# Attention followed by two gated MLPs on one core: key chunks in another order, weights-times-values products in three groups per head pair instead of five

## The chip, the cores and the metric

One core of a Trainium2 chip. The metric is the device time of one launch in microseconds. Engines are called as in the profile: PE (matmul) and PEld (its weight load), DVE, ACT, POOL, SP (the queue that issues the DMAs).

## What is computed

Attention over 4 batches of 8 heads with 576 positions and 64 channels, all in float32, then two MLPs on the 2304 x 512 result:

```python
scores = scale * np.matmul(q, k.transpose(0, 1, 3, 2))
thresh = np.max(scores, axis=-1, keepdims=True) - tau
scores = np.where(scores >= thresh, scores, -1000000000.0)
attn = softmax(scores)
x = np.matmul(attn, v)                  # heads side by side: 2304 x 512
x = (s * relu(x @ w_in) ** 2 + b) @ w_out
h = x @ w2_in;  out = (h * tanh(softplus(h))) @ w2_out
```

## The kernel before

The 32 heads are worked on as 16 **pairs** `pr` of two heads, four pairs to a batch. The 2 x 576 query rows of a pair make nine tiles `ti` of 128 rows (tile 4 holds the last 64 rows of both heads). `scores` (L238) computes one tile: four matmuls into `S` (eight for tile 4), a pass of DVE that gives the negated scores `ns` and their extremum, the exponential on ACT into `e`, and a `finish` on DVE one tile later that applies the threshold and sums. After tiles 1, 4 and 8 POOL divides the finished tiles by their sums (L279).

The weights must then be turned so that keys lie on the partitions. The 2 x 576 key columns of a pair are nine **chunks** of 128 (0 to 3 head 0, 5 to 8 head 1, chunk 4 the last 64 keys of head 0 beside the first 64 of head 1). `weights_t` (L285) transposes one chunk on PE: five transposes into the one PSUM buffer `T`, which ACT copies to an SBUF tile `te` (L302; six buffers). Chunk 4 needs all nine tiles of the pair. `product` (L305) multiplies with the values: `product(c)` takes chunk c for head 0 and chunk c + 5 for head 1 (chunk 4 for both), in four matmuls named A to D here: half 0 head 0, half 0 head 1, half 1 head 0, half 1 head 1. Each writes 64 of the 128 output columns of the array, head 0 the lower and head 1 the upper half. Every float32 matmul of this line leaves two rows in the trace, so a product leaves eight. The five products of a pair add up in one PSUM tile `pv`, which `split_x` (L316) takes out as `x[pr]`.

`attention` (L326) is a generator over tiles k. At tile k it emits the scores of tile k, the transposes of chunk number k - LAG, with LAG 7, and then the product that the chunk of the tile before made possible: after chunk 4 product 4, after chunks 5 to 8 products 0 to 3. At tiles 2 and 4 the next pair's keys and queries are prepared, at tile 8 the next pair's values are loaded.

The first MLP, `moe1` (L386), runs in blocks of one batch (four pairs): groups of 12 matmuls of 288 columns (L405). Its first block starts when `x[0]` to `x[3]` exist and splits its weights on the way (`wp`); later blocks load them (`w`). `run` (L584) interleaves the two generators by the estimated cost that each has emitted, attention inside `tc.high_priority(offset=200)` (L643). The fourth block of the first MLP and then the second MLP (`moe2`, L471) follow when attention is over.

What stands on each engine in which order is not the order of emission. The kernel is built with `schedule_with_timeline_sim=True` (L713): a scheduler gives each engine a fixed order of instructions, by readiness and priority.

Of the kernel before, what the change touches and what calls it, by code (L numbers as in the profile page):

```python
# [19 lines left out]
class Fused:  # L20
# [305 lines left out]
    def attention(self):  # L326

        nc = self.nc  # L330
        N = 9 * self.B * self.NP
        LAG = 7
        for n in "kq":
            self.load_raw(0, n)
        nc.sync.dma_start(self.tau_c, self.tau.partition_broadcast(P))
        nc.sync.dma_start(self.s_c, self.s.partition_broadcast(P))
        nc.sync.dma_start(self.b_c, self.b.partition_broadcast(P))
        self.load_raw(0, "v")
        for n in "kq":
            self.prep_qk(0, n)  # L340
        fin = todo = None
        tes = {}
        for k in range(N + LAG + 2):
            pr, ti = divmod(k, 9)
            if k < N:
                nxt = self.scores(pr, ti)
                if fin:
                    fin()
                fin = nxt
                yield 550  # L350
                if pr + 1 < self.B * self.NP and ti in (2, 4, 8):
                    if ti == 8:
                        self.load_raw(pr + 1, "v")
                    else:
                        self.prep_qk(pr + 1, "kq"[ti // 2 - 1])
                        yield 500
            elif fin:
                fin()
                fin = None
            j = k - LAG  # L360
            if 0 <= j < N:
                prj, ci = divmod(j, 9)
                tnew = self.weights_t(prj, ci)
                yield 550
            if todo:
                tp, tc, te = todo
                tes[tc] = te
                if tc == 4:
                    self.product(tp, 4, (te, te), True, False)
                    yield 490  # L370
                elif tc > 4:
                    self.product(tp, tc - 5, (tes[tc - 5], te), False, tc == 8)
                    yield 970
                if tc == 8:
                    self.split_x(tp)
            todo = (prj, ci, tnew) if 0 <= j < N else None


# [7 lines left out]
    def moe1(self, b):  # L386
# [79 lines left out]

        for layer, qf, part in ORDER:
            yield from (layer1, layer2)[layer](qf, part)


    def moe2(self, rest):  # L471
# [5 lines left out]
        def load(bi):  # L477
            n = 512 if bi < 4 else 256
            ys[bi] = [], [], n
            for e in range(4):  # L480
                for i, tag in enumerate(("xh", "xl")):
                    t = self.xp.tile([P, n], F32R, tag=tag, name=f"y2{bi}_{e}_{i}")
                    nc.sync.dma_start(t.bitcast(F32), self.yT[bi, e, i] if bi < 4 else self.yrem[e, i])
                    ys[bi][i].append(t)
# [42 lines left out]
        def output(bi, fc):  # L527
            gh, gl = gs.pop((bi, fc))
            n = ys[bi][2]
            w = self.w2["o", fc // 4]  # L530
            terms = [(gh, 0), (gh, 1), (gl, 0)]
            todo = [(i, t) for i in range(3) for t in range(n // 128)]
            if fc == 15:
                todo.sort(key=lambda it: it[1])
            for i, t in todo:
                if fc == 0 and i == 0:
                    outs[t] = self.op.tile([P, 512], F32, tag=f"o{t}", name=f"o{bi}_{t}")
                g, wl = terms[i]
                nc.tensor.matmul(outs[t], g[:, t * 128:t * 128 + 128], w[:, wl, fc % 4, :],  # L539
                                 start=(fc == 0 and i == 0), stop=(fc == 15 and i == 2))  # L540
            if fc < 15:
                return
            for t in range(n // 128):
                o = self.yp.tile([P, 512], F32, tag=f"y{t}", name=f"os{bi}_{t}")
                if t % 2:
                    nc.vector.tensor_copy(o, outs[t])
                else:
                    nc.scalar.copy(o, outs[t])
                if bi < 4:

                    dst = self.out[bi * 576:bi * 576 + 512, :].rearrange("(j c) e -> c j e", c=4)[t]
                    nc.sync.dma_start(dst, o)
                else:
                    for i in range(2):
                        r0 = (2 * t + i) * 576 + 512
                        nc.sync.dma_start(self.out[r0:r0 + 64, :], o[64 * i:64 * i + 64, :])

        LAG = 3
        load(0)
        prev = None  # L560
        n = len(work)
        for i in range(n + LAG):
            if i < n:
# [12 lines left out]
            prev = cur  # L576
            if i >= LAG:
                output(*work[i - LAG])
            for _ in range(2):
# [4 lines left out]
    def run(self, ctx):  # L584
# [5 lines left out]
        def pool(stack, name, bufs, **kw):  # L590
# [16 lines left out]
        att = self.attention()  # L607
        w1 = self.split_all([f for u in ORDER for i in range(2) for f in self.w1_pieces(u[0], u[1], 2 * u[2] + i)],
                            self.pre, ("raw", "ra"), bufs=3)
# [61 lines left out]

HALVES = [slice(0, 64), slice(64, 128)]

ORDER = [(0, 0, 0)]
for _q in range(4):
    ORDER += [(0, _q, 1)] + ([(0, _q + 1, 0)] if _q < 3 else []) + [(1, _q, 0), (1, _q, 1)]

# [40 lines left out]
```

## Time and profile before

| | |
|---|---|
| median of 3 runs | 1219.41 us (1215.17 to 1219.55) |
| the profiled execution | 1216.89 us |
| its span, first to last instruction | 1215.1 us |
| PE busy / PEld busy | 1153.1 us (95%) / 983.9 us (81%) |
| DVE / ACT / POOL busy | 868.4 / 592.5 / 657.9 us |
| mean granted clock of PE | 0.984 |
| first and last row of the products (L313) | 45.6 us and 656.7 us |
| first matmul of the first MLP | 131.5 us |

The profile is one execution. A row of the timeline merges neighbours of one kind on an engine; its first number is the start of the first, and the difference between two such starts is what the first kind took of PE. A matmul's own duration is longer than that, since matmuls overlap.

### The profile page before, as it was taken

What the parts mean: (1) busy time and instruction counts of PE and PEld (TensorE: products, weight loads), DVE (VectorE), ACT (ScalarE), POOL (GpSimd) and SP (SyncE); (2) the same over time, 40 slices, a digit from 0 to 9 for tenths busy, and PEclk for the clock granted to TensorE, in tenths of its full rate; (3) what the DMA queues carried; (4) which work ended last, traced back from release to release, by engine and by line L of the source; (5) the groups of instructions that cost most, each with busy time, mean ns of one, the idle gap of its engine ahead of it and who ended that gap; (6) DMA issues with size and microseconds to landing.
All of it is one profiled execution on the core that took longest, in us unless ns stands there. A gap on an engine that the chain in (4) does not pass through costs nothing.

```text
span 1215.1 us, 20290 instructions
## 1 busy us (share of the span) xinstructions
PE 1153.1 (95%) x7104; PEld 983.9 (81%) x7104; DVE 868.4 (71%) x1585; ACT 592.5 (49%) x1153; POOL 657.9 (54%) x841
## 2 busy tenths in 40 slices
PE   5888999999899999999999999988999999999998
PEld 4666878877788998988998999966888888888886
DVE  5888777878885465664652799799977676767865
ACT  4666666575555544455532575453433333344332
POOL 5566777786644343335431354346755655555654
PEclk8989999999999999999999999989999999999999
DMA  5556466576585445474433898842130020020000
GB/s 129 157 142 180 111 210 183 168 208 175 175 288 165 144 144 165 127 227 132 131 99 111 288 323 267 293 148 70 36 104 1 1 70 1 8 97 1 18 1 35
DMA packets 123671, 161.88 MB, mean 133 GB/s; under 512 B 57392, under 2 KB 78896, under 8 KB 123568
## 3 DMA queue, kind: packets, MB, share of 16 engines
q1 hardware_dynamic: 123568, 160.58, 43.2%
q8 instruction: 56, 0.92, 0.3%
q14 instruction: 47, 0.39, 0.1%
HBM read 107.48 MB, written 30.93 MB: 114 GB/s over the span
## 4 chain that ended last, share of the span: by engine, by line
PE 59%; DVE 13%; DMA 10%; POOL 6%; issue 5%; ACT 4%; SPq 2%; DVEq 0%; ACTq 0%; POOLq 0%
PE o L539 12%; PE h L405 11%; PE y L405 9%; PE pv L313 6%; PE hp L495 6%; PE hm L495 6%; PE S L254 5%; DMA wraw<-in_moe_w_in_dram 5%; PE T L291 4%; DMA wraw<-in_moe_w_out_dram 3%; DVE d L512 3%; POOL e L279 2%; DVE wa L67 2%; DVE wa L68 2%; DVE wa L66 2%
## 5 line engine op out<-in xcount | busy, mean ns | idle before, releaser
L512 DVE RECIPROCAL d<-d 128x512 f32<-128x512 f32 (+1 forms) x80 | 242.0, 3025 | 0.0
L405 PE MATMUL y<-gh,w 128*128 128x288 f32 x768 | 164.0, 299 | 2.7 <-DVE y L452 2.7
L405 PE MATMUL h<-xh,w 128*128 128x288 f32 x768 | 164.8, 300 | 1.3 <-DMA w<-w 1.0
L269 DVE SCALAR_TENSOR_TENSOR e<-ns,st,e 128x576 f32<-128x576 f32 x128 | 120.9, 948 | 45.5 <-ACT e L265 30.1
L260 POOL TENSOR_SCALAR st<-st,tau_c 128x1 f32<-128x1 f32 x144 | 60.9, 424 | 165.9 <-DVE ns L258 151.0
L539 PE MATMUL o<-w2o,g2h 128*128 128x512 f32 x576 | 149.7, 395 | 0.1
L258 DVE TENSOR_SCALAR_CACHE_REDUCE ns<-S 128x576 f32<-128x576 f32 x144 | 107.8, 752 | 55.6 <-PE S L254 54.9
L279 POOL TENSOR_SCALAR e<-e,st 128x576 f32<-128x576 f32 x128 | 126.4, 997 | 31.3 <-DVE st L274 28.9
L405 PEld LDWEIGHTS y<-gh,w 128*128 128x128 f32 x768 | 125.7, 188 | 10.2 <-issue 4.4
L265 ACT ACTIVATE e<-ns,st 128x576 f32<-128x576 f32 x128 | 98.9, 776 | 70.6 <-DVE ns L258 59.5
L405 PEld LDWEIGHTS h<-xh,w 128*128 128x128 f32 x768 | 125.7, 188 | 8.5 <-issue 5.7
L539 PEld LDWEIGHTS o<-w2o,g2h 128*128 128x128 f32 x576 | 107.1, 188 | 24.8 <-ACT g2h L519 0.6
L302 ACT COPY te<-T 128x576 f32<-128x576 f32 x144 | 91.3, 634 | 72.1 <-PE T L296 64.9
L429 POOL TENSOR_TENSOR gl<-rr,gh 128x288 fp32r<-128x288 f32 x96 | 81.0, 850 | 73.8 <-DVE rr L428 63.2
L495 PE MATMUL hp<-y,w2i 128*128 128x512 f32 (+1 forms) x480 | 113.6, 380 | 6.1 <-DVE t L511 6.0
L516 POOL TENSOR_TENSOR t<-t,d 128x512 f32<-128x512 f32 (+1 forms) x80 | 94.9, 1186 | 40.5 <-DVE d L512 40.3
L523 POOL TENSOR_TENSOR g2l<-t,g2h 128x512 fp32r<-128x512 f32 (+1 forms) x80 | 95.5, 1193 | 38.4 <-ACT g2h L519 36.1
L405 PE MATMUL y<-gl,w 128*128 128x288 f32 x384 | 113.7, 296 | 1.5 <-DVE gl L429 1.5
L405 PE MATMUL h<-xl,w 128*128 128x288 f32 x384 | 113.8, 296 | 0.0
L495 PE MATMUL hm<-y,w2i 128*128 128x512 f32 (+1 forms) x480 | 110.1, 373 | 3.1 <-DVE t L511 3.0
L254 PE MATMUL S<-KH,Q 128*128 128x288 f32 x320 | 101.6, 333 | 11.8 <-DVE ns L258 4.0
L291 PE MATMUL T<-ident,e 128*128 128x128 f32 x576 | 99.1, 281 | 13.6 <-ACT te L302 9.3
(100 smaller groups left out, 2481.8 us busy)
## 6 DMA issues: line engine op xcount, KB each, us to landing
w<-w SPq DMA_DIRECT2D x96, 512.0 KB, 4.2
wraw<-in_moe_w_in_dram SPq DMA_DIRECT2D x64, 256.0 KB, 3.9
w<-wp SPq DMA_DIRECT2D x32, 512.0 KB, 4.0
wraw<-in_moe_w_out_dram SPq DMA_DIRECT2D x64, 256.0 KB, 4.3
KH<-hik SPq DMA_DIRECT2D x60, 144.0 KB, 2.5
y<-yT SPq DMA_DIRECT2D x32, 256.0 KB, 4.1
KL<-lok SPq DMA_DIRECT2D x30, 144.0 KB, 2.7
rawq<-in_q_dram SPq DMA_DIRECT2D x32, 128.0 KB, 3.1
```

The costliest lines, as they stand in the source:

```text
L254: nc.tensor.matmul(so, Q[:, c0:c0 + 128], kt[:, ks], start=(i == 0), stop=(i == len(terms) - 1))
L258: nc.vector.tensor_scalar(ns.rearrange("p (h n) -> p h n", h=2), sv, -0.125, 3.0e38, op0=ALU.mult, op1=ALU.min, accum_out=nm[:, c1])
L265: nc.scalar.activation(e, ns, AF.Exp, bias=nm[:, c1], scale=-1.0)
L269: nc.vector.scalar_tensor_tensor(e, ns, nthr[:, c1], e, op0=ALU.is_le, op1=ALU.mult, accum_out=sm[:, c1])
L279: nc.gpsimd.tensor_scalar(t, t, rinv[:, j:j + 1], u[:, j:j + 1], op0=ALU.mult, op1=ALU.add)
L291: nc.tensor.transpose(T[:, i * 128:i * 128 + 128], self.es[pr, i, "pair"][:, o:o + 128], self.ident)
L405: nc.tensor.matmul(acc[:, :n], w[:, wl, c], rhs[c][xl][:, ts], start=(i == 0), stop=(i == 11))
L495: nc.tensor.matmul(hp[:, :n], w[:, wl, kc, fs], yy[kc], start=(i == 0), stop=(i == 11))
L512: nc.vector.reciprocal(d, d)
L516: nc.gpsimd.tensor_tensor(t, t, d, op=ALU.mult)
L523: nc.gpsimd.tensor_tensor(gl, t, gh.bitcast(F32), op=ALU.subtract)
L539: nc.tensor.matmul(outs[t], g[:, t * 128:t * 128 + 128], w[:, wl, fc % 4, :], start=(fc == 0 and i == 0), stop=(fc == 15 and i == 2))
```

## The change

The chunks of a pair are transposed in the order 0, 1, 4, 5, 6, 2, 7, 3, 8 instead of 0 to 8, nine tiles behind the scores instead of seven. The products are emitted in three groups: 4 and 0 after chunk 5, 1 and 2 after chunk 7, 3 after chunk 8. Values are loaded for the first two pairs at the start, and then for pair tp + 2 as soon as pair tp has been taken out of `pv`. `yield` costs of a product are 970 throughout (490 for product 4 before).

```diff
-        LAG = 7
+        LAG = 9
...
-        self.load_raw(0, "v")
+        for pr in range(2):
+            self.load_raw(pr, "v")
...
-                if pr + 1 < self.B * self.NP and ti in (2, 4, 8):
-                    if ti == 8:
-                        self.load_raw(pr + 1, "v")
-                    else:
-                        self.prep_qk(pr + 1, "kq"[ti // 2 - 1])
-                        yield 500
+                if pr + 1 < self.B * self.NP and ti in (2, 4):
+                    self.prep_qk(pr + 1, "kq"[ti // 2 - 1])
+                    yield 500
...
-                prj, ci = divmod(j, 9)
+                prj, cj = divmod(j, 9)
+                ci = CHUNKS[cj]
...
-                if tc == 4:
-                    self.product(tp, 4, (te, te), True, False)
-                    yield 490
-                elif tc > 4:
-                    self.product(tp, tc - 5, (tes[tc - 5], te), False, tc == 8)
+                for c in PRODUCTS.get(tc, ()):
+                    self.product(tp, c, (tes[c], tes[c + 5 if c < 4 else 4]), c == 4, c == 3)
                     yield 970
                 if tc == 8:
                     self.split_x(tp)
+                    self.load_raw(tp + 2, "v")
...
+CHUNKS = (0, 1, 4, 5, 6, 2, 7, 3, 8)
+PRODUCTS = {5: (4, 0), 7: (1, 2), 8: (3,)}
```

## Rows read from the trace of the kernel before

**Rows 1.** The page: busy time, share of the span and instructions of each engine.

```profile
PE 1153.1 (95%) x7104; PEld 983.9 (81%) x7104; DVE 868.4 (71%) x1585; ACT 592.5 (49%) x1153; POOL 657.9 (54%) x841
```

**Rows 2.** Windows: stretch, its us, busy us per engine (instructions), PE clock, DMA.

```profile
0.00:131.00 131.00, 103.69 (x620) 76.74 (x621) 100.27 (x278) 76.31 (x129) 76.56 (x134) 0.91 0.58 150
131.00:350.00 219.00, 205.06 (x1442) 175.57 (x1440) 171.70 (x430) 133.99 (x283) 160.34 (x226) 0.98 0.62 184
350.00:657.00 307.00, 306.15 (x2257) 272.86 (x2255) 165.51 (x404) 149.00 (x275) 122.94 (x174) 1.00 0.50 153
```

**Rows 3.** Waits of PE, 350 to 657 us: total us, times, longest us.

```profile
PE h L405 <- DMA w<-w: 0.4, 1, 0.4
PE T L291 <- ACT te L302: 0.4, 2, 0.2
```

**Rows 4.** The products: all by line L313; groups by line, 131 to 350 and 350 to 657 us.

```profile
L313 PE MATMUL pv<-te,rawv x640: 406/406/742, 45.6 to 656.7; 128*64 128x288 f32 x160
...
L313 PE MATMUL pv<-te,rawv 128*64 128x288 f32 x204 | 33.5, 419 | 0.0
...
L313 PE MATMUL pv<-te,rawv 128*64 128x288 f32 x280 | 47.3, 420 | 0.0
```

**Rows 5.** Timeline of PE, products of one pair: start us, us, what, number.

```profile
368.62 0.27 PE L296 MATMUL T<-ident,E 128*128 128x128 f32 x1
368.82 1.67 PE L313 MATMUL pv<-te,rawv 128*64 128x288 f32 x10
370.42 0.40 PE L405 MATMUL h<-xh,w 128*128 128x288 f32 x1
...
373.35 0.27 PE L296 MATMUL T<-ident,E 128*128 128x128 f32 x1
373.55 1.19 PE L313 MATMUL pv<-te,rawv 128*64 128x288 f32 x8
374.67 0.53 PE L405 MATMUL h<-xh,w 128*128 128x288 f32 x2
...
386.63 0.70 PE L313 MATMUL pv<-te,rawv 128*64 128x288 f32 x2
387.25 0.40 PE L254 MATMUL S<-KH,Q 128*128 128x288 f32 x1
```

**Rows 6.** Timeline of PE, a chunk's last transpose with no product behind it.

```profile
401.21 0.27 PE L296 MATMUL T<-ident,E 128*128 128x128 f32 x1
401.24 0.38 PE L405 MATMUL y<-gh,w 128*128 128x288 f32 x1
```

**Rows 7.** Timeline of PE, last products ahead of the first MLP.

```profile
127.97 1.19 PE L313 MATMUL pv<-te,rawv 128*64 128x288 f32 x8
...
130.36 1.18 PE L313 MATMUL pv<-te,rawv 128*64 128x288 f32 x6
131.47 0.41 PE L405 MATMUL h<-xh,wp 128*128 128x288 f32 x1
```

**Rows 8.** Timeline of ACT, the copy of chunk 5 of the pair of rows 5.

```profile
368.93 0.64 ACT L302 COPY te<-T 128x576 f32<-128x576 f32 x1
```

**Rows 9.** Timeline of SP, the load of the second pair's values.

```profile
15.79 0.95 SPq L173 DMA_DIRECT2D rawv<-in_v_dram  x2
```

**Rows 10.** Timeline of PE, transposes of a chunk 4.

```profile
405.44 0.27 PE L291 MATMUL T<-ident,e 128*128 128x128 f32 x1
...
406.07 0.27 PE L291 MATMUL T<-ident,e 128*128 128x128 f32 x1
```

**Rows 11.** Waits of PE, 130 to 350 us and 0 to 130 us.

```profile
PE S L254 <- DVE ns L258: 2.5, 5, 0.9
...
PE T L291 <- ACT te L302: 7.8, 9, 2.1
```

**Rows 12.** Waits of the SP queue, whole span.

```profile
SPq L173 <- PE pv L313: 9.7, 6, 4.2
```

## The prediction

> **What bounds the kernel now.** I began with busy time on the page: PE 95%, DVE 71% [rows 1]. A mean over stages decides nothing, so the windows came next. From 350 to 657 us PE is busy 306 of 307 us [rows 2], and the waits view finds 0.8 us there that PE spent on others [rows 3]: attention and the first MLP share an engine that never stops, and a microsecond added to it is a microsecond of the launch. From 131 to 350 us PE is idle 14 of 219 us, before that 27 of 131 [rows 2]; added work can hide there in part. The last product row starts at 656.7 [rows 4], so what follows is only shifted. The products lie 280 rows in the full stretch, 204 in the middle one, the rest of 640 before [rows 4]: at 40 rows per pair 7 pairs, 5 and 4.
>
> **What a run of products costs.** The timeline around one pair gives it, by starts. Without a product the next matmul starts 0.03 us after a chunk's last transpose [rows 6]. With one, the product starts 0.20 us after it, and the next matmul comes 1.60 us later behind ten rows, 1.12 behind eight, 0.62 behind two [rows 5], 1.11 behind six [rows 7]. Set against the 0.03, a run costs 1.77, 1.29, 0.79 and 1.28 us for ten, eight, two and six. Two full steps of PE more are 0.48 us (ten against eight), so a step is 0.24 us: two rows where a head 0 matmul stands beside a head 1 matmul, one where it stands alone. Four steps are 0.97 us, so of an eight-row run 0.32 us is entering and leaving. Fewer runs save 0.32 us each; single matmuls waste half a step's array.
>
> **How the order arises.** The front says that a scheduler lays down PE's order by readiness and priority. Three readings show what it does. A run of ten stands where product 4 has eight rows of its own [rows 5]: the other two are matmul A of product 0, whose operand, chunk 0, was ready, although it is emitted a tile later. The second pair's values are loaded at 15.79 us [rows 9], although that load is emitted at tile 8. The transposes of a chunk 4 stand singly [rows 10], each as its operand came. So attention's instructions go as soon as their operands are there, ahead of their place in the program and of the MLP. Matmul B does not overtake: it needs the second chunk, and C and D stay behind it.
>
> **The change, part by part.** (1) The groups. Emission in groups does not hold matmuls back; only operands do. A chunk's copy is done about 0.95 us after its last transpose starts (368.62 to 369.57) [rows 5, 8], and that copy frees both the one buffer T for the next chunk's transposes and the products of the copied chunk. So products follow the next transposes, as at 373.55 [rows 5]. I walk the new order with this rule, naming the run by the chunk transposed just before it:
>
> after 5: 4A 4B 4C 4D 0A, ten rows;
> after 6: 0B 0C 0D 1A, eight;
> after 2: 1B 1C 1D, six (chunk 6 is copied, chunk 2 not yet, so 2A cannot follow);
> after 7: 2A, two;
> after 3: 2B 2C 2D, six;
> after 8: 3A, two;
> after the next pair's 0: 3B 3C 3D, six.
>
> Seven runs: 1.77 + 1.29 + 3 x 1.28 + 2 x 0.79 = 8.48 us. Before, ten, eight, eight, eight and six: 1.77 + 3 x 1.29 + 1.28 = 6.92 us. Each pair pays 1.56 us more, 25.0 us over 16 pairs.
>
> How much reaches the end: all of it in the seven pairs of the full stretch, 10.9 us. In the five pairs of the middle stretch 7.8 us meet 14 us of PE idling; no idle is as regular as the runs, and the waits of score matmuls, for one, come to 2.5 us in all [rows 11], so I take three quarters, 5.9, between 0 and 7.8. In the first four pairs 6.2 us meet 27 us, 7.8 of which are transposes waiting for the copy of T [rows 11], just where the new short runs would stand; I take a third, 2.1, between 0 and 6.2.
>
> (2) LAG 9. Chunk 4 keeps its distance from the scores (third chunk at lag 9 against fifth at lag 7), but now six chunks follow it instead of four, so `x[3]` comes two tiles later. Ahead of the first MLP a tile takes 2.39 us (127.97 to 130.36) [rows 7]: 4.8 us in which PE has only attention and is idle as in the first stretch, 21% of the time. The attention work done meanwhile is not lost, so I take 1.0 us, between 0 and 4.8. At the end of attention two more tiles come behind the last scores, covered by MLP matmuls that PE still has after 656.7: nothing.
>
> (3) Value loads. Two pairs are loaded at the start: SP issues the second pair's four DMAs some 6 us earlier than the 15.79 of now [rows 9], with the next pair's keys and queries behind them, which nobody needs for many microseconds: nothing, at most the 2 us of issuing. Later loads stand behind the last product of the pair that frees the buffer. SP already waits there, 9.7 us in six waits, the longest 4.2 [rows 12], since readiness has put the load there today; weights and the moves of keys and queries queue behind it, and PE waited 0.4 us for DMA in the full stretch [rows 3]. Nothing, between 0 and 4.2 us.
>
> (4) Buffers. At most five of the six `te` are held (for example 1, 6, 2, 7 and 3), against six before, so no wait appears. The `e` tiles of a pair come free two tiles later, still ahead of the pair after next. Transposes, copies, scores and all other instructions keep their number.
>
> Sum: 10.9 + 5.9 + 2.1 + 1.0 = 19.9 us on the profiled execution's 1216.89: 1236.8. That execution is 2.5 us under the median of the runs shown and 1.7 over the lowest; I add 1 and say 1238. With the lower bounds (10.9) it is 1228, with the upper ones (10.9 + 7.8 + 6.2 + 4.8) 1247.
>
> **The rivals.** *The groups stand as written* (faster). It needs a scheduler that keeps 1B until chunk 7 is copied, against the ten-row run and the early load [rows 5, 9]. Then three runs: 4 and 0 with 1A, ten steps, 1.77 + 4 x 0.24 = 2.73 us; 1 and 2 with 3A, eight steps, 1.29 + 0.97 = 2.26; six rows 1.28. That is 6.27, or 0.65 less per pair: 7 x 0.65 + 0.75 x 5 x 0.65 + 4 x 0.65 / 3 less the 1.0 of LAG is 6.9 us, so 1210, between 1206 and 1217. The point that decides: whether a product whose chunks are copied goes before its emission by two tiles, as it goes by one today.
>
> *Five or six runs*: 2A and 3A join a neighbour because the build sees a copy done earlier or later than I read. Extra 0 to 0.8 us per pair: 1217 to 1228.
>
> *The weight loads are PE's real limit* (no change). PEld is busy 273 of the 307 us [rows 2], 34 us free, more than the 10.9 asked for; then only the first stretch pays, and the time is about 1220. Against it, every row of the runs moves the next matmul's start, and 0.8 us of waits leave no gap to fill [rows 3, 5]. The Trainium skill, Perfetto Trace Analysis, section Identifying the Most-Contended Engine, advises reading PE's headroom from weight loads instead of matmul busy time; by that rule the added runs would be absorbed, and the trace agrees only as far as matmul ends being modelled.
>
> *The tail is uncovered* (slower still): attention falls so far behind the MLP that the last `x` comes when the third block has nothing left. It decides once the last product runs more than the MLP work still standing behind 656.7 later; each microsecond beyond costs one: 1245 to 1260.
>
> **How the numbers follow.** Seven runs 0.69, groups as written 0.12, five or six runs 0.10, weight loads 0.05, tail 0.04. Half a per cent, about what a measurement of this kernel tells from no change, is 6.1 us: 1213.3 and 1225.5. Faster: 0.11 of the groups and 0.01 of the five or six, 0.12. Same: 0.01, 0.06, the 0.05 of weight loads and 0.03 of seven runs that hide well, 0.15. Slower: the rest, 0.73. The likeliest case has 1228 to 1247 for itself; down to 1214 the range takes in the fewer runs and the weight loads and leaves out most of the groups and of the tail, some 0.17.
>
> **What would show it.** On the timeline of PE, runs of L313 per pair: ten, eight, six, two, six, two, six if I am right; about 18, 16 and 6 if the groups stand, and then I am wrong. The steps 0.20, 1.12 and 0.62 should return unchanged. PE's waits in the shared stretch should stay near 0.8 us; if they grow, the extra time is a wait and not runs. The first MLP should start near 136 us instead of 131.5, and SP should wait for `pv` on L173 about as long as now.

## The result, and the profile after

The changed kernel took 1231.63 us (median of 4 runs, 1230.97 to 1233.74), the kernel before beside it on the same chip 1219.48 us. The ratio is 1.0112, 95% interval 1.0085 to 1.0138: slower, as forecast, some 6 us less so than the 1238 named. The profiled execution took 1230.97 us, that of the kernel before 1216.89: the two profiles lie 14.1 us apart, the medians 12.2.

The page of the changed kernel, its head and its busy times, to be held against [rows 1]:

```profile
span 1228.8 us, 20284 instructions
...
PE 1174.9 (96%) x7104; PEld 991.7 (81%) x7104; DVE 868.8 (71%) x1585; ACT 593.3 (48%) x1153; POOL 658.8 (54%) x841
```

PE has the same 7104 instructions and is busy 21.8 us longer; PEld moved by 8 and the other three by under 1. The line that pays shows when the groups by line of both kernels are laid side by side. The products over the whole span, first of the kernel before, then of the changed one (line, operation, count; busy us, mean ns; idle before):

```profile
L313 PE MATMUL pv<-te,rawv 128*64 128x288 f32 x640 | 106.9, 424 | 0.0
```

```profile
L313 PE MATMUL pv<-te,rawv 128*64 128x288 f32 x640 | 128.9, 424 | 0.0
```

The same 640 rows with the same mean duration of one fill 22.0 us more. The rows did not become slower; fewer of them overlap. How they stand is read from the timeline of PE, one pair in the full stretch of the changed kernel (start, us, what; the matmul behind each run is shown, for its start):

```profile
431.74 0.27 PE L296 MATMUL T<-ident,E 128*128 128x128 f32 x1
431.95 1.67 PE L313 MATMUL pv<-te,rawv 128*64 128x288 f32 x10
433.55 0.40 PE L402 MATMUL y<-gh,w 128*128 128x288 f32 x1
...
436.79 1.19 PE L313 MATMUL pv<-te,rawv 128*64 128x288 f32 x8
437.91 0.40 PE L402 MATMUL y<-gh,w 128*128 128x288 f32 x1
...
441.96 1.19 PE L313 MATMUL pv<-te,rawv 128*64 128x288 f32 x6
443.08 0.54 PE L402 MATMUL y<-gh,w 128*128 128x288 f32 x2
...
446.50 0.70 PE L313 MATMUL pv<-te,rawv 128*64 128x288 f32 x2
447.13 0.40 PE L402 MATMUL h<-xh,w 128*128 128x288 f32 x1
...
451.31 1.18 PE L313 MATMUL pv<-te,rawv 128*64 128x288 f32 x6
...
455.56 0.70 PE L313 MATMUL pv<-te,rawv 128*64 128x288 f32 x2
...
460.24 1.19 PE L313 MATMUL pv<-te,rawv 128*64 128x288 f32 x6
```

Ten, eight, six, two, six, two, six: seven runs instead of the five of [rows 5]. Line numbers past 350 are three lower here, so L402 is the L405 of before.

The windows of the changed kernel, the three stretches of [rows 2], and then two around the fourth block of the first MLP:

```profile
0.00:131.00 131.00, 107.45 (x603) 79.05 (x605) 101.14 (x282) 76.04 (x127) 78.73 (x134) 0.95 0.58 150
131.00:350.00 219.00, 210.00 (x1437) 175.98 (x1436) 176.49 (x424) 132.59 (x280) 158.63 (x222) 0.99 0.62 190
350.00:657.00 307.00, 307.00 (x2202) 270.99 (x2202) 161.64 (x407) 147.12 (x274) 121.90 (x178) 1.00 0.49 148
657.00:695.00 38.00, 38.00 (x270) 32.55 (x269) 11.95 (x27) 12.90 (x25) 3.19 (x4) 1.00 0.46 144
695.00:807.00 112.00, 105.64 (x777) 103.22 (x776) 97.82 (x233) 63.37 (x170) 50.41 (x48) 1.00 0.82 285
```

In 350 to 657 us the first column of counts says what the change costs: 2202 matmuls where [rows 2] has 2257, in an engine that was full before and is full now. Ahead of it PE idles less: 23.55 us instead of 27.31 up to 131, 9.00 instead of 13.94 from 131 to 350. The corresponding windows of the kernel before around the fourth block, which starts there at 685.5 us and here at 695.8:

```profile
657.00:685.00 28.00, 26.43 (x196) 25.96 (x196) 14.92 (x34) 9.96 (x24) 6.81 (x9) 1.00 0.65 211
685.00:793.00 108.00, 104.60 (x775) 102.86 (x774) 95.50 (x228) 61.94 (x165) 44.55 (x44) 1.00 0.86 293
```

**Where the time went.** I added up PE's steps from one matmul's start to the next, idle taken out, by kind. Up to the start of the fourth block (taken as the 2305th matmul of the first MLP, since neighbouring blocks overlap by some matmuls), products and transposes together take 217.4 us instead of 194.6 (+22.8); idle falls by 11.2; the rest changes by -1.3, so that block starts 10.3 us later. It then lasts 111.0 us instead of 107.1 (+3.9, of which 3.0 are idle). What follows it is 0.4 us shorter up to the last matmul. That makes 13.8, and the spans differ by 13.7 us (1228.8 less 1215.1).

### The profile page after: what moved, and what is told of

It reads as the page before. It is cut to its first block, busy times and chain, and to the rows that moved or that the text cites. A ratio compares the mean times of both kernels' runs of the same rounds, so it can differ in the third digit from the quotient of the medians.

```text
span 1228.8 us, 20284 instructions
## 1 busy us (share of the span) xinstructions
PE 1174.9 (96%) x7104; PEld 991.7 (81%) x7104; DVE 868.8 (71%) x1585; ACT 593.3 (48%) x1153; POOL 658.8 (54%) x841
## 4 chain that ended last, share of the span: by engine, by line
PE 68%; DVE 13%; issue 6%; DMA 5%; POOL 4%; ACT 2%; SPq 1%; DVEq 0%; ACTq 0%; POOLq 0%
PE h L402 14%; PE o L536 12%; PE y L402 11%; PE pv L313 8%; PE S L254 6%; PE hp L492 6%; PE hm L492 5%; PE T L291 4%; DMA wraw<-in_moe_w_out_dram 3%; DVE d L509 3%; DVE wa L67 2%; DVE wa L66 2%; DMA wraw<-in_moe_w_in_dram 2%; DVE wa L68 2%; POOL e L279 1%
## 5 line engine op out<-in xcount | busy, mean ns | idle before, releaser
L402 PE MATMUL y<-gh,w 128*128 128x288 f32 x768 | 164.5, 300 | 3.4 <-ACT gh L424 2.1
L402 PE MATMUL h<-xh,w 128*128 128x288 f32 x768 | 164.4, 299 | 1.2 <-DVE y L449 1.2
L269 DVE SCALAR_TENSOR_TENSOR e<-ns,st,e 128x576 f32<-128x576 f32 x128 | 113.5, 890 | 48.1 <-ACT e L265 39.0
L279 POOL TENSOR_SCALAR e<-e,st 128x576 f32<-128x576 f32 x128 | 127.2, 1004 | 34.3 <-DVE st L274 33.7
L402 PEld LDWEIGHTS h<-xh,w 128*128 128x128 f32 x768 | 125.4, 188 | 13.1 <-issue 7.9
L402 PEld LDWEIGHTS y<-gh,w 128*128 128x128 f32 x768 | 125.9, 188 | 11.6 <-issue 5.3
L313 PE MATMUL pv<-te,rawv 128*64 128x288 f32 x640 | 128.9, 424 | 0.0
L536 PEld LDWEIGHTS o<-w2o,g2h 128*128 128x128 f32 x576 | 107.1, 188 | 24.7 <-ACT g2h L516 0.6
L402 PE MATMUL y<-gl,w 128*128 128x288 f32 x384 | 114.4, 298 | 1.8 <-DVE gl L426 1.7
L402 PE MATMUL h<-xl,w 128*128 128x288 f32 x384 | 113.9, 297 | 0.0
```

Of the source, the lines that this page charges most:

```text
L269: nc.vector.scalar_tensor_tensor(e, ns, nthr[:, c1], e, op0=ALU.is_le, op1=ALU.mult, accum_out=sm[:, c1])
L279: nc.gpsimd.tensor_scalar(t, t, rinv[:, j:j + 1], u[:, j:j + 1], op0=ALU.mult, op1=ALU.add)
L313: self.nc.tensor.matmul(self.pv[HALVES[h], hf * HB:hf * HB + 288], v[:, h, c, :], tes[h][:, hf * 288:hf * 288 + 288], start=first, stop=last)
L402: nc.tensor.matmul(acc[:, :n], w[:, wl, c], rhs[c][xl][:, ts], start=(i == 0), stop=(i == 11))
```

## The experiments

Each carries the median, and the ratio to the kernel before on the same chip with its 95% interval. "Runs" is the number of unbroken runs of L313 on PE; "product time" is PE's steps in products and transposes up to the fourth block, added up as above.

### The lag and the loads alone: the old order

```diff
-CHUNKS = (0, 1, 4, 5, 6, 2, 7, 3, 8)
-PRODUCTS = {5: (4, 0), 7: (1, 2), 8: (3,)}
+CHUNKS = tuple(range(9))
+PRODUCTS = {4: (4,), 5: (0,), 6: (1,), 7: (2,), 8: (3,)}
```

> Lag of nine and the early value loads of the change, with the chunks in the old order 0 to 8 and the products emitted singly. Theory (the time is in the number and length of the runs of products): five runs per pair of ten, eight, eight, eight and six rows as before, L313 busy near 107 us, and the time of before within 0.3% (1215 to 1223 us). Rival (two tiles more between scores and products delay the first MLP and the end of attention): first MLP matmul and last product come as late as in the changed kernel and the time is 1225 us or more.

Measured: 1220.67 us, 1.0019 (1.0002 to 1.0037); 88 runs, as before, and 193.1 us of product time against 194.6. The first MLP starts at 132.4 us instead of 131.5. So the lag of nine and the early value loads together are worth 0.2 to 4.5 us, and the new order with its groups is the rest.

### The new order, each product emitted by itself

```diff
-PRODUCTS = {5: (4, 0), 7: (1, 2), 8: (3,)}
+PRODUCTS = {4: (4,), 5: (0,), 6: (1,), 7: (2,), 8: (3,)}
```

> The changed kernel with its new chunk order, but each product emitted alone after the chunk that completes it, not in groups. Theory (only readiness of operands sets the runs, emission in groups does nothing): seven runs per pair of ten, eight, six, two, six, two, six rows, L313 busy near 129 us, the time of the changed kernel within 0.3% (1228 to 1235 us). Rival (the groups change something): a time at least 4 us away from the changed kernel's.

Measured: 1232.4 us, 1.0115 (1.0088 to 1.0141), 122 runs and 216.6 us of product time. The changed kernel has 121 and 217.4. The theory held. Emission in groups does nothing that shows in the time: take it out, and the same seven runs per pair are left, and a median 0.8 us away.

### Half of the extra runs: chunk 2 ahead of chunk 6

```diff
-CHUNKS = (0, 1, 4, 5, 6, 2, 7, 3, 8)
+CHUNKS = (0, 1, 4, 5, 2, 6, 7, 3, 8)
```

> The changed kernel with chunk 2 moved ahead of chunk 6 (0, 1, 4, 5, 2, 6, 7, 3, 8): by readiness six runs per pair of ten, eight, eight, six, two and six rows, one single matmul instead of two. Theory (time follows the cost of the runs): PE pays 1.77 + 2 x 1.29 + 2 x 1.28 + 0.79 = 7.70 us per pair, half of the change's extra 1.56, so about half of its 12 us: 1223 to 1228 us. Rival (lag or lateness of x): as the changed kernel, 1230 us or more.

Measured: 1224.17 us, 1.0049 (1.0031 to 1.0067), 104 runs, product time 204.5 us, as the theory had it. The products in the groups by line of this kernel:

```profile
L313 PE MATMUL pv<-te,rawv 128*64 128x288 f32 x640 | 117.1, 421 | 0.0
```

Half of the 33 extra runs, 10.2 of the 22.0 us on the line, a little under half of the loss: the cost goes by runs.

### The groups held together by force

The scheduler's `issue_after` keeps a product back until the last transpose emitted so far stands ahead of it; `last_t` is that transpose (the last instruction of `weights_t`).

```diff
-                    self.product(tp, c, (tes[c], tes[c + 5 if c < 4 else 4]), c == 4, c == 3)
+                    with self.tc.issue_after(self.last_t.ins):
+                        self.product(tp, c, (tes[c], tes[c + 5 if c < 4 else 4]), c == 4, c == 3)
```

> The changed kernel with its three groups held together: each product may stand on PE only behind the last transpose emitted before it. Theory: three runs per pair of sixteen, sixteen and eight rows, 20 steps, 2.26 + 2.26 + 1.29 = 5.81 us per pair, 1.11 less than before, 17.8 us of PE in all; of the change's added 22 us of product time some 0.6 reached the end, so about 10 us under before: 1205 to 1213 us, L313 busy near 92 us. Rival (the new order and lag cost by themselves, whatever the runs): 1222 us or more.

Measured: 1204.74 us, 0.9895 (0.9872 to 0.9918). Faster than both kernels, and the fastest of all that ran; just under the 1205 to 1213 expected, since the product time fell by 20.3 us where 17.8 were expected. One pair on its timeline of PE, and its products by line:

```profile
429.81 0.27 PE L296 MATMUL T<-ident,E 128*128 128x128 f32 x1
430.01 2.16 PE L313 MATMUL pv<-te,rawv 128*64 128x288 f32 x16
432.11 0.53 PE L403 MATMUL h<-xh,w 128*128 128x288 f32 x2
...
442.30 2.16 PE L313 MATMUL pv<-te,rawv 128*64 128x288 f32 x16
444.39 0.40 PE L403 MATMUL h<-xl,w 128*128 128x288 f32 x1
...
450.20 1.19 PE L313 MATMUL pv<-te,rawv 128*64 128x288 f32 x8
451.32 0.40 PE L403 MATMUL h<-xh,w 128*128 128x288 f32 x1
```

```profile
L313 PE MATMUL pv<-te,rawv 128*64 128x288 f32 x640 | 90.8, 416 | 0.0
```

Three runs of whole products: 16, 16 and 8. By the prediction's prices they cost 2 x (1.29 + 4 x 0.24) + 1.29 = 5.8 us a pair, 2.7 less than the 8.48 of seven runs, 43 over 16 pairs. The product time is 174.3 us, 43.1 less than in the changed kernel. In the full stretch its window shows PE with 149 more matmuls than the changed kernel, in the same time:

```profile
350.00:657.00 307.00, 307.00 (x2351) 284.17 (x2351) 168.03 (x419) 150.77 (x280) 119.25 (x178) 1.00 0.51 153
```

### The old order, its five products held

The same edit on both product calls of the kernel before.

> The kernel before, lag 7 and old chunk order, with each product held behind the last transpose emitted before it, so that no matmul A runs ahead with the product before. Theory (runs and steps): five runs per pair of eight rows, 20 steps instead of 22, 5 x 1.29 = 6.45 us instead of 6.92, 0.47 less per pair and some extra splits less, 7 to 10 us of PE in all, of which about 0.6 reached the end in the runs so far: 1212 to 1216 us. Rival (holding itself delays attention's chain and eats the gain): 1217 us or more.

Measured: 1218.86 us, 1.0009 (0.9997 to 1.0021): a miss. With 81 runs the product time is 186.7 us, 7.9 less than before, yet the launch gained nothing. The first MLP starts at 134.3 us instead of 131.5, the last product stands at 678.5 instead of 656.7, and the fourth block takes 113.4 us instead of 107.1. The fourth block starts only 2.1 us earlier (683.4 instead of 685.5), since PE idles 4.1 us more ahead of it, and then lasts 6.3 us longer: what was saved in the products was given back there. Why the held products end so much later, with less work on PE, I did not settle.

### The new order, held in two groups

```diff
-PRODUCTS = {5: (4, 0), 7: (1, 2), 8: (3,)}
+PRODUCTS = {6: (4, 0, 1), 8: (2, 3)}
```

on top of the three held groups.

> The three held groups made two: products 4, 0 and 1 after chunk 6, products 2 and 3 after chunk 8, held behind the last transpose. Theory (runs and steps): two runs per pair of 24 and 16 rows, 20 steps, 3.23 + 2.26 = 5.49 us, 0.32 less per pair than three held groups, 5 us of PE, 3 us of time: 1200 to 1204 us. Rival (long blocks of products make attention end later, and the fourth MLP block, which took 117 us with three held groups against 107 before, gets longer still): 1205 us or more, with the time added in the fourth block.

Measured: 1214.09 us, 0.9968 (0.9952 to 0.9983): a miss, 9 us slower than three groups. The rival named such a time, but not its place: the fourth block takes 115.0 us, less than the 117.1 of three groups. There are only 37 runs, but the product time, 173.1 us, is hardly below the 174.3 of three groups, and the first MLP starts at 136.5 us instead of 130.5. PE does not idle longer ahead of it (24.6 us against 25.7); in this profile its clock is lower. The windows from 0 to 131 us, first of three groups, then of two (the third figure from the end of a row is the mean granted clock):

```profile
0.00:131.00 131.00, 100.24 (x620) 77.71 (x621) 101.40 (x285) 77.15 (x130) 80.12 (x136) 0.90 0.58 150
```

```profile
0.00:131.00 131.00, 101.74 (x597) 78.98 (x598) 97.42 (x270) 74.39 (x126) 78.66 (x132) 0.86 0.58 150
```

PE is busy 1.5 us longer and has done 23 instructions fewer. From 80 to 100 us the granted clock is 0.83 here and 1.00 in three groups: after waits of 1.04 and 0.47 us for the divided weights (from L279), score matmuls that had stepped by 0.13 us (88.35 to 88.48) step by 0.24 (93.17 to 93.41), the lower of the two clock levels. But this is one execution. Its mean clock, 0.975, is the lowest of the seven of this kernel, five of which had 0.983 to 0.986; and the three at 0.986 still took 1212.1 to 1212.2 us, 5 us more than the slowest of three groups (1207.0 at 0.984). So the clock is not shown to be what makes two groups slower, and the cause stays open.

### The first MLP held back to attention's pace

A list `t_hist` takes the last transpose of each chunk; in the loop that interleaves the two generators:

```diff
-                c = next(mo, None)
+                with tc.issue_after(self.t_hist[-9]):
+                    c = next(mo, None)
```

On the changed kernel, to ask whether attention's late end is the loss:

> The changed kernel with the same seven runs per pair, but the first MLP's matmuls may stand on PE only behind the transposes emitted nine tiles before them, so that attention lags less and its last product has about 180 MLP matmuls of blocks one to three behind it, as in the kernel before (198; 50 in the changed kernel). Theory (the runs' PE time carries the loss up to the fourth MLP block, the late end of attention adds only what the fourth block takes longer, 111 us against 107): fourth block starts at 693 to 698 us as in the changed kernel and takes 107 to 109, total 1225 to 1230 us. Rival (the late end of attention is the whole loss, since the second MLP's weights are split only from then on): 1216 to 1222 us.

Measured: 1242.53 us, 1.0196 (1.0174 to 1.0218), worse than either theory had it. The same on the three held groups:

> The three held groups with the same bound on attention's lag: 192 matmuls of blocks one to three behind the last product instead of 24. Theory: the fourth block starts near 669 us as with the three held groups and takes 107 to 109 us instead of 117, total 1194 to 1199 us. Rival (PE now waits for attention's chain, which it had hidden behind MLP matmuls): idle time of PE between 131 us and the fourth block grows beyond 20 us and the total stays at 1203 us or more.

Measured: 1214.35 us, 0.997 (0.9955 to 0.9985), slower than without the hold, as the rival had it: PE idles 20.9 us between 131 us and the fourth block, where it idled 15.4 without the hold. Both give the fourth block back its length (107.8 and 106.7 us), but its start moves later by more: 711.7 us instead of 695.8, and 683.3 instead of 668.7. Over what stands ahead of the block the first has 7.1 us more PE idle than the changed kernel, 3.9 more in scores, 3.4 in MLP steps and 2.2 in transposes. So the MLP was kept back and attention hardly came forward: its last product moved from 688.7 to 684.6 us. That the late end is all of the loss finds no support. Why scores and transposes take longer steps under this hold I did not settle.

### The second MLP's weights later, nothing else

The kernel before; its weight splits for the second MLP start only at step 24 of the fourth block's generator, behind a load of that block (`loads` lists the loads of L397):

```diff
-            if i % 2 == 0:
-                next(w2, None)
+            if i % 2 == 0 and i >= 24:
+                with tc.issue_after(self.loads[2 * 32 + 5].ins):
+                    next(w2, None)
```

> The kernel before, attention and its products untouched; only the loads of the second MLP's weights are held on SP behind the sixth weight load of the fourth MLP block, so that their splitting starts near 690 us instead of 670, as late as in the changed kernel. Theory (a late start of that splitting lengthens the fourth block and what follows): fourth block starts at 685 us as before and takes 112 to 120 us instead of 107, total 1223 to 1232 us. Rival (the splitting is hidden behind the fourth block): total below 1220 us.

Measured: 1222.37 us, 1.0042 (1.0028 to 1.0056). The first of these loads is issued at 689.9 us instead of 669.7; the fourth block starts where it did (684.2 us) and lasts 117.5 us instead of 107.1. Some 4 us of these 10 come back later (PE's idle after the block falls from 9.3 to 5.4 us): the launch is 0.4% longer, some 5 us, just short of the 1223 to 1232 expected and above the rival's 1220. What PE waits for in the block is the work of ACT and DVE between its two layers; the waits of PE in the fourth block, first of the kernel before, then of this one:

```profile
PE y L405 <- DVE y L452: 1.6, 1, 1.6
PE y L405 <- DVE gl L429: 1.5, 1, 1.5
```

```profile
PE y L406 <- ACT gh L428: 3.5, 2, 3.3
PE h L406 <- DVE y L453: 2.0, 2, 1.5
PE y L406 <- DVE gl L430: 1.6, 2, 0.8
```

### The kernels together

The lead is from the first load of the second MLP's weights to the start of the fourth block (negative: the load comes later).

| kernel | runs | product time | last product | lead | fourth block | ratio |
|---|---|---|---|---|---|---|
| before | 88 | 194.6 | 656.7 | 15.8 | 107.1 | 1 |
| changed | 121 | 217.4 | 688.7 | 8.3 | 111.0 | 1.0112 |
| lag and loads alone | 88 | 193.1 | 657.5 | 16.0 | 107.8 | 1.0019 |
| products singly | 122 | 216.6 | 693.9 | 4.0 | 113.1 | 1.0115 |
| half of the runs | 104 | 204.5 | 680.7 | 7.1 | 115.0 | 1.0049 |
| three groups held | 54 | 174.3 | 665.1 | 3.9 | 117.1 | 0.9895 |
| five held | 81 | 186.7 | 678.5 | 5.4 | 113.4 | 1.0009 |
| two groups held | 37 | 173.1 | 672.5 | 2.9 | 115.0 | 0.9968 |
| changed, MLP held back | 122 | 219.2 | 684.6 | 16.6 | 107.8 | 1.0196 |
| three groups, MLP held back | 56 | 180.9 | 656.1 | 15.1 | 106.7 | 0.997 |
| weights later | 88 | 193.1 | 657.5 | -5.7 | 117.5 | 1.0042 |

Two costs stand beside each other. Product time goes by runs: between the changed kernel, half of the runs, the kernel before and three held groups it is 0.6 to 0.8 us for each (12.9 us for 17, 9.9 for 16, 20.3 for 34). The kernel with two held groups doesn't follow: 17 runs fewer than with three, and 1.2 us. The length of the fourth block goes by the lead: 107 to 108 us at 15 and more, 111 to 118 below 9, there not in step with it.

## Why the prediction was right, and where its sizes were off

**The price of a run** held: 0.21 us from the last transpose (431.74) to the product, 1.60 behind ten rows, 1.12 behind eight and six, 0.63 behind two, against 0.20, 1.60, 1.12, 1.11 and 0.62.

**The order** held run by run, and with it the rule that readiness, not emission, sets it: the kernel with products emitted singly has the same seven runs per pair on PE.

**The PE time added**: predicted 25.0 us, measured 22.8 in products and transposes. In all there are 121 runs, nine more than seven a pair, and before 88, eight more than five; that about cancels. By stretch it is 2.8 us ahead of the first MLP, 8.1 from there to the tenth pair and 12.0 behind, against forecasts of 6.2, 7.8 and 10.9 for four, five and seven pairs.

**The share that reaches the end** is the term that was mis-sized. The prediction let 18.9 of the 25.0 through, with three quarters in the middle stretch and a third in the first. The windows show idle falling by 3.8 us up to 131, 4.9 from 131 to 350, 0.9 in the full stretch and 1.6 behind it: 11.2 us were absorbed, about half of 22.8, where the forecast absorbs 4.1, 1.9, nothing and nothing. The step that failed reads "no idle is as regular as the runs, so I take three quarters, 5.9, between 0 and 7.8". In that stretch the idle gave back 4.9, so that at most 2.9 of the 7.8 passed, within the bounds but near the lower one. In the first stretch the third was near, and the wait that the prediction named did shrink. The waits of PE from 0 to 131 us in the changed kernel, beside the 7.8 us for the copy of T in [rows 11]:

```profile
PE T L291 <- POOL e L279: 7.8, 11, 1.5
...
PE T L291 <- ACT te L302: 1.2, 3, 0.5
```

The wait for the copy fell from 7.8 to 1.2 us (1.0 with the products emitted singly, 5.8 with the lag and the loads alone); that short runs of products now stand in it is argued. The wait for POOL's division there rose from 3.6 to 7.8 us, and it is 7.6 with the lag and the loads alone, so the runs need not be its cause. How much the first stretch absorbs is not settled by one profile: the kernel with products emitted singly, with the same runs, idles 27.1 us up to 131, hardly less than the kernel before, though its idle between 131 us and the fourth block falls from 16.4 to 7.2 us (9.0 in the changed kernel). Its mean granted clock there is 0.91, as in [rows 2]; the changed kernel's profile has 0.95.

**The lag and the loads**: 1.0 us forecast, 0.2 to 4.5 measured, the two not told apart. The first MLP starts at 133.9 us; the prediction said near 136.

**The queue** was wrong. SP was to wait for `pv` about as long as in [rows 12]; the waits of the SP queue in the changed kernel say otherwise:

```profile
SPq L173 <- PE pv L313: 38.9, 13, 13.0
```

With the lag and the loads alone it is 6.3 us, so the new order does it: the pair's last product comes later, and SP stands behind it. PE has no wait of any kind from 350 to 657 us, so nothing was lost there by it.

**The end of attention** was costed at nothing, and this is the other term that was mis-sized. The last product moves from 656.7 to 688.7 us. Its `x` is done at 690.8, and the first matmuls of the fourth block follow at 692.6, among the last of the third, so the third block had not run out and the rival *tail uncovered*, as written, did not happen. But the loads of the second MLP's weights come later. The SP queue, the first of these loads, before and after (the views leave digits out of names, so `in_moe_w_in_dram` stands for the weights of both MLPs):

```profile
669.67 1.28 SPq L59 DMA_DIRECT2D wraw<-in_moe_w_in_dram  x3
```

```profile
687.45 1.89 SPq L59 DMA_DIRECT2D wraw<-in_moe_w_in_dram  x4
```

They move 17.8 us, the block only 10.3. In the kernel before the first of them waits, 13 us behind the last product, until the third block's first layer has read the buffers that it takes (`xp` in `run`); the waits of the SP queue over the whole span:

```profile
SPq L59 <- PE h L405: 2.5, 3, 1.7
```

In the changed kernel that layer is over by 678.5 us, and the first load, at 687.45, waits for nothing: it stands where the fixed order of the queue has it. In all six kernels of the table with a lead from 2.9 to 8.3 it comes 0.2 to 1.3 us ahead of attention's last product. So the loads go with the end of attention by their place in the queue, and why the scheduler puts them there is not shown. More of the splitting then falls into the block, whose DVE is busy 97.8 of 112 us, and PE waits for DVE and ACT there; the waits of PE in the fourth block of the changed kernel:

```profile
PE y L402 <- ACT gh L424: 2.1, 1, 2.1
PE y L402 <- DVE gl L426: 1.7, 2, 1.2
PE h L402 <- DVE y L449: 1.2, 2, 0.9
```

That a late start of these loads does this by itself is shown by the kernel that delays nothing else. That it is the whole of the 3.9 us is argued, not shown: `x` itself is late too, and in the kernel before the fourth block's first matmuls stand among the third's from 677.4 us, 8 us ahead of its start by count, here 3 us. No run delays only `x`.

So 22.8 - 11.2 - 1.3 + 3.9 - 0.4 = 13.8 us stands between the two profiles, against the forecast of 19.9. Of the 6.1 us that the forecast is too high, 5.1 were absorbed beyond it, 2.2 are PE time that the runs did not take, 1.0 was set down for the lag and 1.7 are the rest, less the 3.9 at the end: that the sum came so near is in part luck, since errors of opposite sign met in it.

**The rivals.** *The groups stand as written* needs a scheduler that holds them, and this one doesn't; where they are made to stand, the launch is 1204.7 us, below the 1206 to 1217 given for it. *Weight loads are the real limit* falls: PEld is busy 271 of the 307 us of the full stretch, and yet 55 matmuls fewer fit. The Trainium skill, Perfetto Trace Analysis, section Identifying the Most-Contended Engine, would read 36 us of headroom there; for runs of this kind the trace disagrees, though with three groups held PEld does rise to 284 us. *Five or six runs* was not seen.

## What to carry to other kernels

Ask who decides the order. Where a scheduler goes by readiness, writing work in larger groups changes nothing, or splits them further when a reordering makes operands ready at other times; hold the group explicitly, and count the runs on the timeline afterwards. Then follow what the held or delayed work releases at its end: a stage that finishes later can cost time in the next one through what is queued to come after it, here the loads of the next weights, even though the engine that bounds the kernel has less to do.

## What was not expected of the hardware

- A short run is dear out of proportion. Two rows take 0.63 us of PE and sixteen take 2.09 (442.30 to 444.39): 0.31 us a row against 0.13. The mean duration of a row, 424 and 416 ns, shows nothing of it; only starts do.
- A full PE is not one whose weight loads are full. With three groups held, 149 more matmuls than in the changed kernel stand in the same 307 us, although PE is busy throughout in both, and PEld rises from 271 to 284 us.
- The granted clock is not the same in all executions of one kernel: over the whole launch it is 0.975 to 0.986 with two held groups. In the first 131 us the changed kernel's profile has 0.95 and that of the same runs emitted singly 0.91, as the kernel before. The clock of one stretch in one profile doesn't show what a change does to the clock.
